# A transformer-like stack on one core: the same operations in another written-out order, with buffers handed out in order of release

## The chip, the cores and the metric

The kernel runs on one core of a Trainium2 chip. The metric is the time of one execution on the device, in microseconds (us); the median of several runs counts. One execution of the kernel before was also taken by the hardware profiler, and all rows shown come from that one.

## The reference

Four layers in a row over x of 2048 tokens by 512, all in float32:

```python
def A(x, wqkv, wo):                # 32 heads of 16; window of 8 tokens, every second one back
    q, k, v = split((x @ wqkv))    # 512 -> 3 * 512
    logits[s, w] = q[s] . k[s - 2*w] * 16**-0.5     (s - 2*w < 0 is masked)
    return (softmax(logits) weighted sum of v[s - 2*w]) @ wo

def B(x, w1, w2, w3, w4):
    h = gelu(layernorm(x) @ w1)
    # the four quarters of h's columns are shifted by +1, -1, +2, -2 tokens
    x1 = x + shifted(h) @ w2
    return x1 + gelu(layernorm(x1) @ w3) @ w4       # 512 -> 1792 -> 512

x = x + A(layernorm(x));  x = x + B(layernorm(x))
x = x + A(layernorm(x));  x = x + B(layernorm(x))
```

## The kernel before

**Tiles.** The tokens are cut into 4 blocks of 512, each of 4 tiles of 128. With two passes through A and B there are 8 units, numbered n = 0 to 7. For each unit the program has the stages p1 (normalize x, transpose it, multiply by wqkv, write q, k and v to DRAM), p2 (load q, and k and v with their windows, and do the attention on VectorE: products of 128x2048, reductions, softmax, sums), p3 (multiply by wo, normalize, transpose, multiply by w1, Gelu, shift), p4 (multiply by w2, normalize, transpose) and p5 (the wide MLP in 14 slices: up by w3, Gelu, down by w4 into accumulators). Stages of neighbouring units overlap.

**Precision.** Most products are done on pairs of float16: each operand is a rounded part and a rest, and three products (high by high, high by rest, rest by high) stand for one. So a typical operation on TensorE is a group of 12 matmuls of 128x512. Splitting a tile into the two parts is what much of the work on ScalarE (ACT), VectorE (DVE) and GpSimd (POOL) is: a copy to float16, then a subtraction. In the wide MLP a bank of products is read by three such steps: the Gelu in place (`mm<-mm,s_w`), the high part (`g<-mm,c_g`), and the rest, either on DVE (`g<-mm,c_g,g`) or by a copy on ACT (`f<-mm,c_g`) and a subtraction on POOL.

**The chain of a transposed tile.** A normalization takes a sum of squares on ACT, three tiny steps on POOL (tile `small`, 128x1), the scaling on ACT, the split on ACT and DVE or POOL, and a transposing DMA issued by SP, the queue of nearly all transfers. Only then can TensorE multiply the tile.

**Banks.** PSUM has 8 banks of 128x512, four called `mm` (for products that are evicted at once) and four called `acc` (for sums over many slices). A new group of matmuls into an `mm` bank waits until all steps that read its previous contents are done. The other buffers (`x`, `kv`, `q`, `f32`, `ev`, `g`, `w` and so on) are handed out in the same way from pools of 1 to 11.

**Order.** The program first builds a list of 3513 operations (class `Graph`), each with its engine or a choice of two engines, its estimated cost, what it reads and writes, and the buffers it touches. Nothing of the order is left to a scheduler: `PLACES[k]` is the place of the k-th operation built in one list for all engines, and `OTHER` names the operations that use their second engine. `plan` walks the list in that order, gives each operation its buffers, and the instructions are then issued in it; a helper keeps each engine's instructions in program order. So an engine whose next instruction waits holds up all that stand behind it in its queue. All instructions are issued from one line (L354), so rows of the profile are told apart by their tiles, not by lines.

In the kernel before, `plan` also carries a model of the engines (start times, delays, a port that VectorE and GpSimd share, DMA lanes, table loads, a cold TensorE), whose only use is the choice of buffers: of the free ones it takes that which, by the model, was released first.

Of the kernel before, what the change touches and what calls it, by code (L numbers as in the profile page):

```python
# [227 lines left out]
class Graph:  # L228
# [3 lines left out]
    def __call__(self, key, alts, r=(), w=(), after=(), xfer=0.0, late=0.0):  # L232
# [34 lines left out]
        return o  # L267


LAT, LAT_PE, LAT_SP, LAT_DMA, LEAD, TABLE, COLD = 0.06, 0.35, 0.15, 1.5, 0.85, 1.3, 1.0  # L270
TAIL = (0.165, 0.085, 0.115, 0.0, 0.0)
FREE = (6.5, 1.0, 0.72, 1.2, 0.72)
LANES = 8
GRANT, HELD, SMALL = 0.14, 0.4, ("tiny", "root")
BY_DMA = {"p1": 1, "p2": 1, "p3": 1, "p4": 0}


def plan(ops, slots):
# [9 lines left out]
    for o in sorted(ops, key=lambda o: o.key):  # L288
        assert o.n == 0, "an operation stands before one that it needs"
        e, d, o.fn, cls = o.alts[OTHER.get(o.seq, 0)]  # L290
        begin = o.est
# [1168 lines left out]
```

## Time and profile before

| | |
|---|---|
| median of 3 runs | 1149.2 us (1148.75 to 1150.22) |
| the profiled execution's own time | 1149.52 us |
| its span, first to last instruction | 1147.7 us |
| mean granted TensorE clock | 0.995 |
| TensorE busy | 1121.6 us, 98% |
| VectorE, ScalarE, GpSimd busy | 77%, 54%, 43% |
| DMA | 207.16 MB, mean 180 GB/s |

Busy time is the union of an engine's instructions; a busy TensorE need not run at its peak. "Idle before" is the time in which the engine had nothing to run, and the name behind the arrow is what ended it. A wait for several things is put down to the one that came last.

### The profile page before, as it was taken

The numbers are of one execution on the slowest core, as the hardware profiler recorded it, in microseconds if no ns is written. First come the engines' busy times: TensorE is split into PE (matmuls) and PEld (weight loads), VectorE is DVE, ScalarE is ACT, GpSimd is POOL, SyncE is SP. The second block draws the span as 40 slices with busy tenths as digits, with TensorE's granted clock in tenths as the row PEclk, the third lists the DMA queues.
The fourth block names the chain that finished last, engine by engine and source line by source line (L and its number), as shares of the span: only waits on it lengthen the run. The fifth ranks groups of instructions, "written<-read, shape, count | busy, mean of one in ns | idle before, by whom it ended". The sixth has DMA issues, their size and how long they took to land.

```text
span 1147.7 us, 15205 instructions
## 1 busy us (share of the span) xinstructions
PE 1121.6 (98%) x5236; PEld 526.5 (46%) x5236; DVE 880.8 (77%) x914; ACT 617.6 (54%) x1077; POOL 489.9 (43%) x619
## 2 busy tenths in 40 slices
PE   8999998998999999999999899999999999999998
PEld 6554444443444444444444344444444444444544
DVE  3999999988998998887889787777877989423212
ACT  4975884257754476365554556463545545545322
POOL 4656584156423455255535323444545342324000
PEclk9999999999999999999999899999999999999999
DMA  7789999998988579974488649884767567434323
GB/s 221 192 215 230 244 260 252 239 219 221 241 230 205 116 193 204 243 195 119 108 218 201 158 112 243 197 211 126 170 175 208 154 152 188 110 83 83 102 83 101
DMA packets 247101, 207.16 MB, mean 180 GB/s; under 512 B 134344, under 2 KB 188616, under 8 KB 247024
## 3 DMA queue, kind: packets, MB, share of 16 engines
q1 hardware_dynamic: 245408, 204.42, 71.2%
q10 hardware_dynamic: 1616, 1.77, 0.5%
q8 instruction: 41, 0.67, 0.3%
q14 instruction: 36, 0.29, 0.1%
HBM read 132.64 MB, written 37.87 MB: 149 GB/s over the span
## 4 chain that ended last, share of the span: by engine, by line
PE 55%; DVE 18%; POOL 8%; issue 7%; ACT 6%; DMA 5%; SPq 1%; POOLq 0%; DVEq 0%; ACTq 0%
PE mm L354 38%; PE acc L354 17%; DVE prod L354 10%; POOL small L354 4%; DVE L L354 3%; ACT f L354 2%; ACT junk L354 1%; SPq L354 1%; DMA kv<-kv_d 1%; DVE x L354 1%; POOL f L354 1%; DVE f L354 1%; DVE mx L354 1%; DVE g L354 1%; DMA w<-in_A_x_dram 1%
## 5 line engine op out<-in xcount | busy, mean ns | idle before, releaser
L354 PE MATMUL acc<-w,g 128*128 128x512 f16 (+1 forms) x1260 | 308.3, 393 | 2.0 <-DVE g L354 0.5
L354 PE MATMUL mm<-nT,w 128*128 128x512 f16 (+1 forms) x1344 | 293.5, 372 | 2.1 <-DVE g L354 1.1
L354 PE MATMUL mm<-wq_hl,xt 128*128 128x512 f16 x1008 | 230.4, 384 | 10.3 <-ACT f L354 3.4
L354 PEld LDWEIGHTS <-w 128*128 128x128 f16 x1512 | 141.2, 98 | 158.6 <-issue 7.3
L354 POOL TENSOR_SCALAR small<-small 128x1 f32<-128x1 f32 (+1 forms) x204 | 120.2, 590 | 158.2 <-ACT junk L354 147.0
L354 ACT ACTIVATE mm<-mm,s_w 128x512 f32<-128x512 f32 (+1 forms) x144 | 90.0, 627 | 174.3 <-PE mm L354 173.9
L354 PEld LDWEIGHTS <-g 128*128 128x128 f16 x1176 | 114.5, 98 | 140.4 <-DVE g L354 2.7
L354 DVE TENSOR_TENSOR prod<-kv,L 128x2048 f32<-128x2048 f32 x64 | 150.0, 2344 | 14.6 <-POOL o L354 10.3
L354 PEld LDWEIGHTS <-xt 128*128 128x128 f16 x1008 | 99.2, 99 | 132.3 <-issue 14.7
L354 DVE TENSOR_REDUCE L<-prod 128x128 f32<-128x2048 f32 x64 | 146.0, 2282 | 1.1
L354 DVE TENSOR_TENSOR prod<-kv,q 128x2048 f32<-128x2048 f32 x58 | 139.6, 2407 | 4.2 <-DMA kv<-kv_d 2.6
L354 DVE TENSOR_TENSOR prod<-prod 128x1024 f32<-128x1024 f32 (+1 forms) x114 | 121.5, 1068 | 5.3 <-ACT prod L354 2.8
L354 DVE SCALAR_TENSOR_TENSOR g<-mm,c_g,g 128x512 f16<-128x512 f32 x56 | 41.5, 746 | 78.2 <-ACT g L354 78.1
L354 PE MATMUL mm<-nT,w_hl 128*128 128x512 f16 x384 | 87.2, 380 | 1.8 <-DVE mx L354 1.8
L354 PE MATMUL mm<-w_hl,h 128*128 128x512 f16 x384 | 86.1, 379 | 0.4 <-POOL h L354 0.2
L354 POOL TENSOR_TENSOR g<-f,g 128x512 f16<-128x512 f32 x31 | 48.6, 1569 | 84.7 <-ACT f L354 42.0
L354 PE MATMUL mm<-wo_hl,oT 128*128 128x512 f16 x336 | 74.2, 379 | 0.0
L354 POOL TENSOR_TENSOR small<-small,nhalf 128x1 f32<-128x1 f32 (+1 forms) x104 | 71.1, 684 | 6.3
L354 POOL TENSOR_TENSOR prod<-prod 128x512 f32<-128x512 f32 x17 | 23.9, 1408 | 104.6 <-DVE prod L354 104.6
L354 ACT ACTIVATE g<-mm,c_g 128x512 f16<-128x512 f32 x98 | 66.5, 684 | 2.0
L354 PEld LDWEIGHTS <-oT 128*128 128x128 f16 x426 | 41.4, 98 | 50.4 <-DVE oT L354 1.2
L354 PEld LDWEIGHTS <-w_hl 128*128 128x128 f16 x384 | 37.6, 99 | 48.0 <-issue 4.2
(196 smaller groups left out, 1253.3 us busy)
## 6 DMA issues: line engine op xcount, KB each, us to landing
w<-w SPq DMA_DIRECT2D x210, 256.0 KB
kv<-kv_d SPq DMA_DIRECT2D x112, 352.0 KB
kv_d<-ev SPq DMA_DIRECT2D x112, 128.0 KB
w<-in_B_w_dram SPq DMA_DIRECT2D x42, 256.0 KB
q_d<-ev SPq DMA_DIRECT2D x28, 256.0 KB
w<-g SPq DMA_DIRECT2D x28, 256.0 KB
q<-q_d SPq DMA_DIRECT2D x28, 256.0 KB
x<-x SPq DMA_DIRECT2D x26, 256.0 KB
```

The source lines that it names most:

```text
L354: i = f(*a, **k).ins
```

## The change

Both lists are replaced, and `plan` loses its model: a buffer that is released goes to the end of its pool's list, and the next operation that needs one takes the first of that list. The new lists come from a search outside the program with an event-driven picture of the engines and of the port that VectorE and GpSimd share. No operation is added, removed or resized. 94 of the 3513 operations keep their place in the list. `OTHER` goes from 137 to 151 entries. 132 operations change engine:

| from | to | operations |
|---|---|---|
| DVE | POOL | 51 |
| POOL | DVE | 54 |
| ACT | POOL | 15 |
| POOL | ACT | 9 |
| DVE | ACT | 2 |
| ACT | DVE | 1 |

Of the operations that follow in the text, with their place in their engine's own queue:

| operation | what it is | engine | place before | place after |
|---|---|---|---|---|
| 45 | centring the fourth input tile | POOL, then DVE | 12 | 8 |
| 1278 | product for the wide MLP, unit 1 | PE | 143 | 143 |
| 1639 | tiny normalization step, p4 of unit 2 | POOL | 248 | 260 |
| 1651 | tiny normalization step, p4 of unit 2 | POOL | 251 | 257 |
| 1652 | scaling that reads it | ACT | 388 | 381 |
| 1778 | product by wqkv, unit 5 | PE | 190 | 190 |
| 1823 | copy that frees its bank before | ACT | 390 | 389 |
| 1448 | copy that frees its bank after | ACT | 395 | 385 |
| 1862 | exponential of the attention, unit 5 | ACT | 531 | 531 |
| 2105 | product for the wide MLP, unit 3 | PE | 260 | 259 |
| 2106, 2107, 2108 | Gelu, high part and copy of it | ACT | 532, 533, 534 | 523, 528, 524 |
| 2177 | product by wqkv, unit 6 | PE | 263 | 260 |

The diff, without the two lists' numbers:

```diff
 PLACES = [int(k) for k in """
-49 22 56 77 23 195 3 4 0 1 8 11 14 7 17 19 24 35 36 29 5 16 31 32
...
+68 40 21 101 52 171 3 0 2 1 17 13 19 15 24 26 53 35 29 28 4 8 9 10
...
 def plan(ops, slots):
-    free, latest = list(FREE), {}
-    lane, lanes = 0, [0.0] * LANES
-    pool = {k: [(0.0, j) for j in range(len(v))] for k, v in slots.items()}
-    for o in ops:
+    pool = {k: list(range(len(v))) for k, v in slots.items()}
+    order = sorted(ops, key=lambda o: o.key)
+    for o in order:
         for kind, j in o.lend:
-            pool[kind].remove((0.0, j))
...
-    for o in sorted(ops, key=lambda o: o.key):
+            pool[kind].remove(j)
+    for o in order:
         assert o.n == 0, "an operation stands before one that it needs"
-        e, d, o.fn, cls = o.alts[OTHER.get(o.seq, 0)]
-        begin = o.est
+        o.fn = o.alts[OTHER.get(o.seq, 0)][2]
         for b in o.touch:
             if b.slot is None:
-                got = min(pool[b.kind])
-                pool[b.kind].remove(got)
-                begin, b.slot = max(begin, got[0]), got[1]
+                b.slot = pool[b.kind].pop(0)
                 b.t = slots[b.kind][b.slot]
-        begin = max(begin, free[e])
...
         for kind, j in o.lend:
-            pool[kind].append((o.end + LAT, j))
+            pool[kind].append(j)
         for b in o.touch:
-            latest[b] = max(latest.get(b, 0.0), o.end)
             b.left -= 1
             if b.left == 0:
-                pool[b.kind].append((latest[b] + LAT, b.slot))
+                pool[b.kind].append(b.slot)
```

More of the change, by code (lines that the diff above doesn't have):

```diff
@@ L267, in __call__ @@
         return o
[L270 to L274, printed above, removed]
 BY_DMA = {"p1": 1, "p2": 1, "p3": 1, "p4": 0}
 def plan(ops, slots):
-    free, latest = list(FREE), {}
-    lane, lanes = 0, [0.0] * LANES
-    pool = {k: [(0.0, j) for j in range(len(v))] for k, v in slots.items()}
-    for o in ops:
+    pool = {k: list(range(len(v))) for k, v in slots.items()}
@@ L285, in plan @@
+    order = sorted(ops, key=lambda o: o.key)
+    for o in order:
         for kind, j in o.lend:
-            pool[kind].remove((0.0, j))
-    dma_free, port, wide, table, order = 0.0, 0.0, 0.0, None, []
-    for o in sorted(ops, key=lambda o: o.key):
+            pool[kind].remove(j)
+    for o in order:
         assert o.n == 0, "an operation stands before one that it needs"
-        e, d, o.fn, cls = o.alts[OTHER.get(o.seq, 0)]
-        begin = o.est
+        o.fn = o.alts[OTHER.get(o.seq, 0)][2]
@@ L292, in plan @@
         for b in o.touch:
             if b.slot is None:
-                got = min(pool[b.kind])
-                pool[b.kind].remove(got)
-                begin, b.slot = max(begin, got[0]), got[1]
+                b.slot = pool[b.kind].pop(0)
                 b.t = slots[b.kind][b.slot]
-        begin = max(begin, free[e])
-        if o.xfer:
-            begin = max(begin, *(lanes[(lane + k) % LANES] for k in range(o.parts)))
-            free[e] = begin + d
-            dma_free = max(dma_free, begin + d + LEAD) + o.xfer
-            o.end = dma_free + LAT_DMA + o.late
-            for k in range(o.parts):
-                lanes[lane] = o.end
-                lane = (lane + 1) % LANES
-        else:
-            if e == ACT and cls is not None and cls != table:
-                table = cls
-                d += TABLE
-            if e == POOL:
-                if begin < port:
-                    begin = max(begin, port - GRANT)
-                wide = max(wide, begin) if cls in SMALL else begin + d - GRANT
-            elif cls == "lock":
-                begin = max(begin, wide)
-                port = begin + d
-            if e == PE and begin - free[PE] > COLD and begin > 20.0:
-                d += min(begin - free[PE] - COLD, 2.5)
-            o.end = begin + d + (TAIL[PE] if e == PE else 0.0)
-            free[e] = o.end - TAIL[e]
-            if cls == "root":
-                o.end += HELD
@@ L324, in plan @@
-        order.append(o)
         for s in o.succ:
-            g = s.alts[0][0]
-            s.est = max(s.est, o.end + (LAT if e == g else LAT_PE if g == PE else LAT_SP if g == SP else LAT))
             s.n -= 1
         for kind, j in o.lend:
-            pool[kind].append((o.end + LAT, j))
+            pool[kind].append(j)
         for b in o.touch:
-            latest[b] = max(latest.get(b, 0.0), o.end)
             b.left -= 1
             if b.left == 0:
-                pool[b.kind].append((latest[b] + LAT, b.slot))
+                pool[b.kind].append(b.slot)
```

305 rows, old and new, of tables (OTHER, PLACES) are left out of this document.

## The prediction

> **What bounds the kernel now.** I read the busy shares first, then the table by stretches, then TensorE's own timeline, and last the queues of the engines that its waits name.
>
> The page's first parts (engine, busy us, share of the span, instructions; below, the granted TensorE clock in tenths):
>
> ```profile
> span 1147.7 us, 15205 instructions
> PE 1121.6 (98%) x5236; PEld 526.5 (46%) x5236; DVE 880.8 (77%) x914; ACT 617.6 (54%) x1077; POOL 489.9 (43%) x619
> PEclk9999999999999999999999899999999999999999
> ```
>
> TensorE is the bound: 1121.6 of 1147.7 us, and no product is added or taken away. A new order can win only TensorE's idle time, 26.1 us, and time lost to a low clock; it can lose much more. The stretches show where the idle time lies (stretch, length, then busy us and instructions of PE, PEld, DVE, ACT, POOL, granted clock, DMA share, GB/s):
>
> ```profile
> 0.00:20.00 20.00, 16.17 (x92) 12.91 (x93) 8.24 (x22) 6.51 (x14) 10.57 (x31) 1.00 0.85 251
> 20.00:160.00 140.00, 138.05 (x619) 70.44 (x618) 127.35 (x139) 110.23 (x230) 86.31 (x96) 1.00 0.87 223
> 160.00:180.00 20.00, 17.27 (x73) 7.21 (x72) 19.93 (x27) 16.10 (x26) 15.59 (x22) 0.93 0.88 224
> ...
> 260.00:300.00 40.00, 36.09 (x162) 16.05 (x161) 35.10 (x54) 32.58 (x60) 26.97 (x37) 1.00 0.83 215
> ...
> 440.00:480.00 40.00, 37.49 (x173) 16.62 (x171) 35.39 (x31) 19.72 (x31) 16.27 (x14) 1.00 0.95 219
> ...
> 620.00:660.00 40.00, 36.64 (x158) 15.83 (x157) 30.70 (x26) 21.06 (x32) 17.89 (x19) 0.91 0.64 149
> 660.00:1140.00 480.00, 479.64 (x2339) 221.71 (x2338) 294.75 (x308) 228.96 (x380) 166.62 (x221) 1.00 0.58 147
> 1140.00:1147.70 7.70, 3.24 (x24) 1.57 (x21) 3.27 (x6) 0.71 (x2) 0.00 (x0) 0.93 0.57 170
> ```
>
> Idle are 20 − 16.17 = 3.83 us at the start and 7.70 − 3.24 = 4.46 at the end; so 26.1 − 3.83 − 4.46 = 17.8 us lie between 20 and 1140, of which only 0.36 after 660. The whole second half is full already. Single waits, from TensorE's timeline (start, length, what, count, idle time before it and what ended that):
>
> ```profile
> 17.22 0.66 PE L354 MATMUL mm<-ident,f 128*128 128x128 f32 x4 [1.51 <-POOL f L354]
> ...
> 176.79 7.04 PE L354 MATMUL mm<-wq_hl,xt 128*128 128x512 f16 x24 [2.38 <-DMA xt<-f]
> 184.86 6.01 PE L354 MATMUL mm<-nT,w 128*128 128x384 f16 x36 [1.02 <-ACT ev L354]
> ...
> 267.54 10.52 PE L354 MATMUL mm<-nT,w_hl 128*128 128x512 f16 x48 [1.62 <-DVE mx L354]
> ...
> 320.47 5.34 PE L354 MATMUL mm<-nT,w 128*128 128x512 f16 x24 [1.07 <-DVE g L354]
> ...
> 445.02 5.34 PE L354 MATMUL mm<-wq_hl,xt 128*128 128x512 f16 x24 [1.74 <-ACT ev L354]
> ...
> 638.98 5.28 PE L354 MATMUL mm<-wq_hl,xt 128*128 128x512 f16 x12 [3.36 <-ACT f L354]
> 644.05 3.15 PE L354 MATMUL mm<-nT,w_hl 128*128 128x512 f16 x12
> 647.03 2.75 PE L354 MATMUL mm<-nT,w 128*128 128x512 f16 x12
> ```
>
> An undisturbed group of twelve takes 2.75 us, two take 5.34. After the wait of 3.36 us the next groups took 5.28 and 3.15: 2.53 + 0.40 = 2.93 us lost to the clock (granted 0.91 in that stretch); after the wait of 2.38 the next two took 7.04, 1.70 too much (0.93). After 1.74, 1.62 and 1.07 nothing is lost. So the ceiling is 17.8 + 2.93 + 1.70 = 22.4 us, and at the start no more than 3.83; the last products and the last stores stand alike in both orders.
>
> The Trainium skill ("TensorE: Matmul & The Clock Gate", Part 1, What's actually happening) has the clock halve after an idle window of about 3.4 us and come back after as long a busy one, the window running freely. The wait of 3.36 us agrees; the one of 2.38 is shorter than a window and lost 1.70 all the same, which only the free running allows. If a wait of that length usually cost nothing in clock, the sum below would be 0.85 us poorer (half of 1.70); nothing else hangs on this.
>
> **The change part by part.** All operations are kept; numbers below are those in the order in which the program builds them, places are counted in an engine's own queue by walking both lists. Three things move. (1) Order: of TensorE's 476 operations 258 places hold another one, but blocks only swap with near neighbours. DVE, ACT, POOL and SP are reshuffled at over 90% of places, mostly by a few. (2) 132 operations change engine: 51 from DVE to POOL, 54 back, 15 from ACT to POOL, 9 back, 3 between ACT and DVE. (3) Buffers, PSUM banks above all, go to the next user in the order in which the program releases them, no longer by the planner's release times.
>
> *The wait of 3.36 us at 638.98* (operation 2177). Its bank had belonged to product 2105, whose three ACT steps came last in this queue:
>
> ```profile
> 629.89 0.81 ACT L354 ACTIVATE f<-x,small 128x512 f32<-128x512 f32 x1 [3.43 <-POOL small L354]
> 630.61 0.64 ACT L354 ACTIVATE mm<-mm,s_w 128x512 f32<-128x512 f32 x1
> ...
> 633.73 1.28 ACT L354 ACT_TABLE_LOAD   x1
> ...
> 635.67 1.28 ACT L354 ACT_TABLE_LOAD   x1
> 636.97 0.66 ACT L354 ACTIVATE mm<-mm,s_w 128x512 f32<-128x512 f32 x1
> ...
> 638.25 0.68 ACT L354 ACTIVATE f<-mm,c_g 128x512 f32<-128x512 f32 x1
> ...
> 619.47 0.74 DVE L354 SCALAR_TENSOR_TENSOR x<-mm,s_wo,x 128x512 f32<-128x512 f32 x1
> ```
>
> The product had long been done, but the softmax exponential stood before its Gelu and brought two table loads. In the new queue that Gelu has place 523, not 532, right behind the Gelu of 630.61 and ahead of the exponential (531); its last copy has 524, not 534. And operation 2177 gets another bank, freed by the DVE step of 619.47, done by 620.2; the bank of 2105 goes to a product one group later. The wait should go with its clock loss: −3.36 − 2.93 = **−6.3 us**. What is late next are the normalized tiles of block 4 whose ACT steps now stand behind the Gelu; TensorE meets them at once (the row of 644.05). That goes into the term for new waits.
>
> *The wait of 1.74 at 445.02 and that of 1.07 at 320.47:*
>
> ```profile
> 437.13 4.30 POOL L354 TENSOR_SCALAR small<-small 128x1 f32<-128x1 f32 x3
> ...
> 442.92 0.81 ACT L354 ACTIVATE f<-f,small 128x512 f32<-128x512 f32 x1 [1.11 <-POOL small L354]
> ...
> 444.30 0.67 ACT L354 ACTIVATE ev<-mm,s_kv 128x512 f32<-128x512 f32 x1
> ...
> 306.50 0.69 ACT L354 ACTIVATE ev<-mm,s_kv 128x512 f32<-128x512 f32 x1 [0.38 <-PE mm L354]
> ```
>
> At 445.02 the bank is freed by the copy of 444.30, queued behind the step of 442.92, which waits for POOL. In the new order the longest piece of that POOL stretch (operation 1639) goes from place 248 to 260, behind the step that ACT waits for (257), and another copy frees the bank, at ACT's place 385 instead of 390: **−1.74**. At 320.47 the bank is now one freed by the copy of 306.50, some 12 us early: **−1.07**.
>
> *260 to 300:* idle 40 − 36.09 = 3.91, of it 1.62 at 267.54. The steps in front move by little both ways, and one bank is reused one product earlier; I take half, −1.9, between 0 and −3.9.
>
> *176.79 and 184.86:* 2.38 + 1.70 + 1.02 = 5.1. The first waits for a transposing DMA that stands behind other transfers in SP's queue; its place goes from 180 to 181, and the transfers ahead wait for a DVE step that has place 136, not 144. I take half, −2.5, between 0 and −5.1.
>
> *The start and the moves between engines:*
>
> ```profile
> 11.65 0.49 DVE L354 TENSOR_SCALAR f<-w,mx 128x512 f32<-128x512 f32 x1
> ...
> 15.12 2.04 POOL L354 TENSOR_SCALAR f<-w,mx 128x512 f32<-128x512 f32 x1
> ...
> L354 POOL TENSOR_TENSOR prod<-prod 128x512 f32<-128x512 f32 x17 | 23.9, 1408 | 104.6 <-DVE prod L354 104.6
> ...
> L354 DVE TENSOR_TENSOR prod<-prod 128x512 f32<-128x512 f32 x48 | 35.8, 747 | 1.1
> ```
>
> The step of 15.12, which TensorE awaits for 1.51, goes to DVE, where its like took 0.49: −1.5 (between 0 and −3.8, all that is idle there; another of its kind goes to POOL). The other moves nearly cancel: 51 against 54 change DVE's load by about 3 × 0.75 = 2 us, beside TensorE; I cost them at nothing, since DVE is idle for 480 − 294.75 us after 660, and up to their own 2 us where DVE is full (19.93 of 20 at 160).
>
> *Small waits elsewhere:* 17.8 − 3.36 − 1.74 − 1.07 − 3.91 − 3.40 = 4.3 us, taken as they are. *New waits* are not in this trace: at least 0, at most all that is saved and some more. I take one like that at 176.79 with its clock loss (4.1) and one like that at 320.47 (1.1), 5.2 in all, since a product meets an eviction within one group about as often: among the longer kinds of eviction, three engine steps, I count 9 such reuses of a bank after one product in between, before 12.
>
> Sum: −6.3 − 1.7 − 1.1 − 1.9 − 2.5 − 1.5 + 5.2 = **−9.8 us**. The profiled execution took 1149.5 (span and 1.8 around it), the median is 1149.2: 1149.5 − 9.8 = 1139.7, so **1140 us**.
>
> **The rivals.** *As many new waits as old ones*: the new order is also planned ahead, and a misjudged step anywhere stops TensorE. For it: nearly every place on four queues is new, and bank reuse is hardly looser. Against it: the five largest waits each have a cause that the lists remove. Then the 15.0 us of the terms above come back, 1149.
>
> The Trainium skill ("Perfetto Trace Analysis", Optimizing Scalar/DVE Operations) says that GpSimd and VectorE share a read port, so that shifting work between them might not help. The pair 1408 against 747 ns and the 2.04 us step agree that POOL pays for it; by the rule alone the term at the start would be 0 and the time 1141, within the forecast's case.
>
> *Slower*: POOL's small steps in front of the first MLP block, at 174 us, get 8.8 us more POOL work ahead of them (17.1 in, 8.3 out, by the planner's costs). If that made them late, the wait at 184.86 would grow by 8.8 and lose 2.93 to the clock; with the −2.5 lost as well, −9.8 + 2.5 + 8.8 + 2.9 = +4.4, 1154. It decides from a delay of some 4.4 us on. Against it: POOL idles 140 − 86.31 = 53.7 us before, and after 140 us more is taken out than put in.
>
> *All waits vanish*: −22.4 − 1.5, 1126; against it, four queues are fed by transfers whose landing no order fixes.
>
> **How the numbers follow.** About 0.2% (2.3 us) is what a measurement of this kernel can tell from no change. Chances: the forecast 0.50, all waits vanish 0.10, as many new waits 0.27 (half of it within 0.2%, a third slower, the rest faster), slower by POOL 0.13. Faster 0.50 + 0.10 + 0.05 = 0.65, same 0.13, slower 0.09 + 0.13 = 0.22. The likeliest case's own range: new waits of 0 and both halves won give −9.8 − 5.2 − 4.6 = −19.6, 1130; new waits twice as large and no halves −9.8 + 5.2 + 4.4, 1149. For 8 in 10 the upper end reaches toward the POOL case: 1130 to 1153.
>
> **What would show it.** Right: PE busy 3 to 5 us lower (no clock loss at 640 and 177), mid idle near 10 us, no wait over 2 us between 600 and 660, 445 without its wait. Wrong: a granted clock under 0.95 in a new slice, TensorE waiting for POOL `small` or a transposed tile around 160 to 200, or new waits for `mm` banks after 660, where none were.

## The result, and the profile after

The changed kernel takes 1133.2 us (median of 4 runs, 1128.9 to 1136.1) against 1149.0 for the kernel before in the same comparison: ratio 0.986, 95% interval 0.9827 to 0.9894. Beside the experiments it was run again: 1133.2 (5 runs), ratio 0.9865 (0.9845 to 0.9886). The forecast was 1140, with a range of 1130 to 1153. The profiled execution took 1133.4 us, with a span of 1131.6, 16.1 less than that of before.

The first part of the page, and the stretches (same columns as in the prediction):

```profile
span 1131.6 us, 15180 instructions
...
0.00:20.00 20.00, 16.49 (x84) 13.03 (x85) 8.10 (x20) 6.04 (x14) 9.87 (x25) 0.91 0.90 250
20.00:160.00 140.00, 136.27 (x611) 69.97 (x610) 127.47 (x135) 107.69 (x225) 97.22 (x109) 1.00 0.86 218
160.00:180.00 20.00, 17.19 (x82) 7.77 (x81) 19.90 (x24) 15.40 (x27) 16.07 (x23) 1.00 0.99 263
180.00:260.00 80.00, 79.81 (x337) 39.75 (x336) 76.41 (x76) 33.71 (x63) 24.91 (x29) 1.00 0.92 229
260.00:1124.00 864.00, 862.35 (x4112) 395.77 (x4111) 638.01 (x659) 448.35 (x745) 331.98 (x436) 1.00 0.69 170
```

Behind 180 us TensorE hardly stands: 0.19 us to 260, and 1.65 in the 864 us from there to 1124. Four waits behind 185 were named for the kernel before: those at 638, 445 and 320, and the 3.91 us between 260 and 300. They are gone but for 0.26 us at 275, and nothing of their size has come in their place. Ahead of 180 it is no better than before: 20 to 160 lost 140 − 136.27 = 3.73 us instead of 1.95.

A table cut at the start of the wide MLP's first product (184.86 and 184.87 us in the two kernels) says it most plainly. First the kernel before, then the changed one:

```profile
0.00:184.86 184.86, 175.32 (x795) 92.02 (x796) 160.10 (x190) 135.02 (x272) 115.02 (x147) 0.99 0.87 225
```

```profile
0.00:184.86 184.86, 174.62 (x794) 92.72 (x795) 160.19 (x182) 132.40 (x268) 125.82 (x158) 0.99 0.89 226
```

Up to that product both have run the same 85 operations of TensorE in the same time (the counts differ by one record). So all 16.1 us lie behind it. There the kernel before has 1147.7 − 184.86 = 962.8 us with 1121.6 − 175.3 = 946.3 busy, idle 16.5. The changed one has 946.7 us with 1115.1 − 174.6 = 940.5 busy, idle 6.2. Idle time gave 10.3 us, and the four named waits make 3.36 + 1.74 + 1.07 + 3.91 = 10.1. Busy time gave 5.8, of which 2.93 are the slow products behind 638.98. About half of the other 2.9 is the tails of groups: a group of twelve counts as 2.75 us busy before a wait, and as 2.59 when the next one follows at once. Behind the first product the kernel before has 12 waits and the changed one 3, and 9 × 0.16 = 1.4. For the rest there is no row.

TensorE's own timeline has what is left of waits over 0.7 us, apart from the very first and last:

```profile
9.18 0.66 PE L315 MATMUL mm<-ident,f 128*128 128x128 f32 x4 [1.79 <-POOL f L315]
...
179.32 5.35 PE L315 MATMUL mm<-wq_hl,xt 128*128 128x512 f16 x24 [2.81 <-DMA xt<-f]
184.87 4.06 PE L315 MATMUL mm<-nT,w 128*128 128x384 f16 x24 [0.19 <-DMA nT<-f]
```

Besides these there are 1.64 at 98 us (for POOL's attention output), 1.19 at 121 (for a transposed tile) and 1.00 at 549. The start's wait has only changed owner: operation 45 went to VectorE, but operation 24, the same step on the first tile, went to POOL and took 2.02 us there. The clock of the first 20 us came out lower too (0.91, before 1.00); the prediction had named a new slow slice as a sign against it, and here it lies where nothing was won. The wait at 179, for a transposed tile, is another of those signs. It is longer than its forerunner (2.38), but the two groups behind it took 5.35 us, the undisturbed time.

And ACT's queue around the Gelu that had been late (operations 2106 and 2108 are the rows of 619.08 and 619.77):

```profile
619.08 0.66 ACT L315 ACTIVATE mm<-mm,s_w 128x512 f32<-128x512 f32 x1 [1.41 <-PE mm L315]
619.77 0.69 ACT L315 ACTIVATE f<-mm,c_g 128x512 f32<-128x512 f32 x1
...
624.09 1.28 ACT L315 ACT_TABLE_LOAD   x1
625.38 0.63 ACT L315 ACTIVATE L<-L 128x512 f32<-128x512 f32 x1
```

It runs as soon as its product is there, 18 us earlier than before, and the exponential with its table load follows.

### The profile page after: what moved, and what is told of

It is laid out like the page before. It is cut to its first block, busy times and chain, and to the rows that moved or that the text cites. A ratio compares the mean times of both kernels' runs of the same rounds, so it can differ in the third digit from the quotient of the medians.

```text
span 1131.6 us, 15180 instructions
## 1 busy us (share of the span) xinstructions
PE 1115.1 (99%) x5236; PEld 527.6 (47%) x5236; DVE 872.9 (77%) x915; ACT 611.9 (54%) x1073; POOL 480.1 (42%) x620
## 4 chain that ended last, share of the span: by engine, by line
PE 81%; DVE 6%; DMA 3%; ACT 3%; POOL 3%; issue 1%; SPq 0%; ACTq 0%; DVEq 0%; POOLq 0%
PE mm L315 58%; PE acc L315 24%; DVE prod L315 3%; DMA kv<-kv_d 2%; POOL small L315 1%; DMA xt<-f 1%; ACT junk L315 1%; DVE L L315 1%; ACT f L315 1%; POOL g L315 0%; DVE x L315 0%; ACT x L315 0%; DVE g L315 0%; ACT wq_hl L315 0%; POOL prod L315 0%
## 5 line engine op out<-in xcount | busy, mean ns | idle before, releaser
L315 PE MATMUL mm<-wq_hl,xt 128*128 128x512 f16 x1008 | 225.9, 379 | 4.8 <-DMA xt<-f 4.6
L315 DVE TENSOR_TENSOR prod<-kv,q 128x2048 f32<-128x2048 f32 x58 | 138.2, 2382 | 10.1 <-DMA kv<-kv_d 5.8
L315 POOL TENSOR_SCALAR small<-small 128x1 f32<-128x1 f32 (+1 forms) x204 | 95.4, 468 | 118.8 <-ACT junk L315 106.2
L315 POOL TENSOR_TENSOR g<-f,g 128x512 f16<-128x512 f32 x35 | 51.6, 1480 | 77.3 <-ACT f L315 34.1
L315 POOL TENSOR_TENSOR small<-small,nhalf 128x1 f32<-128x1 f32 (+1 forms) x104 | 81.2, 782 | 6.0
L315 ACT ACTIVATE ev<-mm,s_kv 128x512 f32<-128x512 f32 x56 | 37.7, 682 | 43.8 <-DMA kv_d<-ev 18.4
```

What stands on the lines that cost most here:

```text
L315: i = f(*a, **k).ins
```

## The experiments

My theory after the result: the gain comes from the places of the operations in the queues. Rivals: it comes from the way buffers are given out, or from the engines chosen. The first four runs cross the three parts of the change. The next ones do a single move in one of the two kernels, to see whether a wait has a price of its own. Operations are named by their numbers in building order; a move in the list rewrites `PLACES`, and nothing else.

**The new lists with the old way of giving out buffers.**

```diff
-def plan(ops, slots):            # first in, first out
+def plan(ops, slots):            # the old one, by modelled release times
```

> The new order and the new engines, but buffers given out by the planner's release times as before. Theory (the places in the queues do it, the buffer rule does nothing of size): the banks of the products that stood at 638.98, 445.02 and 320.47 come out the same under both rules, so none of those waits returns; 1134 us, between 1130 and 1138, no wait of TensorE over 3 us in the middle. Rival (the buffer rule does it): most of the 15.8 us come back, 1145 to 1150, with a wait for an mm bank of 2 us or more between 300 and 660.

1133.8 us, ratio 0.9872 (0.9855 to 0.9888). As the theory had it: with the new lists the rule for buffers makes no difference that can be told. The rival falls.

**The old lists with the new way of giving out buffers.**

```diff
-def plan(ops, slots):            # by modelled release times
+def plan(ops, slots):            # first in, first out
```

> The old order and the old engines, with buffers given out first in, first out. Theory (places): the wait of 3.36 us behind the softmax exponential and that of 1.74 at 445 stand again; 1149 us, between 1146 and 1153. Rival (buffer rule): 1133 to 1138, and those two waits are gone.

1164.2 us, ratio 1.013 (1.0115 to 1.0146). Neither theory had that: the two waits stand, as expected (2.53 us at 451 and 2.43 at 650), but the time is 16 us longer than before. ACT's timeline shows where it comes from:

```profile
304.39 0.67 ACT L314 ACTIVATE ev<-mm,s_kv 128x512 f32<-128x512 f32 x1
308.87 0.81 ACT L314 ACTIVATE f<-f,small 128x512 f32<-128x512 f32 x1 [3.81 <-DMA nT<-f]
...
438.82 0.81 ACT L314 ACTIVATE f<-x,small 128x512 f32<-128x512 f32 x1 [2.93 <-DMA xt<-f]
```

A normalization is given an `f` tile that a transposing DMA still reads. First in, first out goes by the order in which the list lets buffers go, and a DMA that stands early in the list ends late. With the old rule the same step began at 304.05, without a wait. TensorE then stands 3.30 us at 323 and 3.96 at 468, for steps queued behind these. Matched product by product with the kernel before, it is 10.6 us late at 500 us and 14.8 at the end. What is lost after 500 us was not followed row by row, though two more such waits for transposing DMAs stand on ACT there (2.06 us at 701, 2.24 at 947). So the rule is not free. The new lists fit it, the old ones don't.

**The new order with the old engines.**

```diff
-OTHER = ...    # 151 entries, the new list
+OTHER = ...    # 137 entries, the list of before; PLACES and plan stay new
```

> The new order and the new buffer rule, but every operation on the engine it had before (132 move back). Theory (places): the waits of 638, 445 and 320 stay away, the first centring step is on VectorE again (its wait of 1.79 us goes), but queues were ordered for the other engines, so some small waits appear; 1136 us, between 1131 and 1142. Rival (engines do it): 1146 to 1150.

1184.5 us, ratio 1.0307 (1.0283 to 1.0331): 51 us slower than the changed kernel, and slower than before. Here my theory was wrong, and so was its rival in that form. Two rows of VectorE and one of TensorE show one of the places:

```profile
125.43 4.48 DVE L314 TENSOR_TENSOR prod<-kv,L 128x2048 f32<-128x2048 f32 x2
129.84 0.68 DVE L314 TENSOR_TENSOR f<-f,f 128x512 f16<-128x512 f32 x1
```

```profile
133.71 6.66 PE L314 MATMUL mm<-wq_hl,xt 128*128 128x512 f16 x24 [5.67 <-DMA xt<-f]
```

The rest of a split (682, 129.84 us) had its input from ACT's step of 119.28, but on VectorE it stands in the list behind the attention's products, and it starts some 10 us late. In the new lists it belongs to POOL. There, in the changed kernel, it ran at 112.89 us, and POOL stood idle for 2.20 us before it and for 4.96 behind it. The loads of the two engine lists hardly differ (VectorE busy 874.0 us here and 872.9 in the changed kernel, GpSimd 489.4 and 480.1); the places are made for one of them.

**The old order with the new engines.**

```diff
-OTHER = ...    # 137 entries, the list of before
+OTHER = ...    # 151 entries, the new list; PLACES and plan stay old
```

> The old order and the old buffer rule, with the new engines. Theory (places): the exponential still stands before the Gelu, so the wait near 638 stands, and POOL steps come at places made for VectorE; 1151 us, between 1147 and 1157. Rival (engines do it): 1134 to 1140.

1156.1 us, ratio 1.0063 (1.0048 to 1.0078). As the theory had it, with the wait at 641.62 grown to 4.62 us. The four runs together: alone, neither the order nor the engines win anything (36 and 8 us slower than before); together they win some 15, with either rule for buffers. So the theory of the places is half right: what the places win, they win only with the engines they were made for. Two mixtures were not run: the new order with the old engines and the old rule, and the old order with the new engines and the new rule.

**The kernel before with the exponential behind the Gelu.**

```diff
 # the list, by operation numbers
-2365 2356 2366 1861 1891 1862 ... 2106 ... 2107 2108 2177
+2365 2356 2366 1861 1891 ... 2106 ... 2107 2108 1862 2177
```

> The kernel before with one operation moved: the softmax exponential of the attention unit stands behind the three ACT steps of the Gelu, not ahead of them; all buffers are given out as before. Theory (the wait of 3.36 at 638.98 and its clock loss of 2.93 came from this one place): the wait is under 0.5 us, granted clock 1.00 in the stretch 620 to 660, 1142.5 us, between 1140 and 1145, all of it still there at the end since nothing waits after 660. Rival (the wait moves on): the next products, on the normalized tiles of block 4, wait instead, and 1146 to 1150 comes out.

1148.4 us (10 runs), ratio 1.0007 (0.9997 to 1.0017). The rival holds. TensorE's and VectorE's timelines:

```profile
638.78 2.75 PE L354 MATMUL mm<-nT,w_hl 128*128 128x512 f16 x12 [0.69 <-DMA nT<-f]
...
649.43 2.75 PE L354 MATMUL mm<-wq_hl,xt 128*128 128x512 f16 x12 [2.72 <-DVE g L354]
```

```profile
646.42 2.29 DVE L354 TENSOR_TENSOR prod<-kv,L 128x2048 f32<-128x2048 f32 x1 [0.84 <-POOL o L354]
648.63 0.74 DVE L354 SCALAR_TENSOR_TENSOR g<-mm,c_g,g 128x512 f16<-128x512 f32 x1
```

The wait of 3.36 is gone, but 0.69 us stand at the next product and 2.72 some 11 us behind that, 3.41 in all. The second is the wait of product 2197 for its bank. The step that frees it (2116, the row of 648.63) has its input at 645.5 and stands behind attention sums on VectorE. While TensorE was held up by ACT, it came too late to notice.

**The same, and that step of VectorE moved ahead of the sums.**

```diff
 # on top of the move above
-1867 1868 1869 1870 2116
+1867 2116 1868 1869 1870
```

> The kernel before with two operations moved: the exponential behind the Gelu as in the run with one move, and VectorE's gated product, which TensorE then awaited for 2.72 us at 649.43, ahead of the attention sums that stood in front of it. Theory (a wait behind one queue covered a wait behind the next; both queues have to be changed): no wait over 1 us between 620 and 660, and 2.7 us less than with one move alone, 1145.5 us, between 1143.5 and 1147. Rival (the stretch is held by still another chain): a third wait within 20 us, 1147.5 to 1149.

1145.8 us (11 runs), ratio 0.9981 (0.9972 to 0.999). The theory holds to 0.3 us: no wait over 0.7 us stands between 620 and 660 (39.32 of 40 us busy), and 2.6 us are won by the medians. The traces agree: matched product by product, TensorE gains 2.9 us between 630 and 655 on the kernel with one move. Two queues had to be changed for one wait; the second move without the first was not run.

**The kernel before with the eviction of 445 moved up.**

```diff
 # ACT's queue, by operation numbers
-1640 1641 1652 1653 1823
+1640 1641 1823 1652 1653
```

> The kernel before with one operation moved: the eviction that TensorE awaits at 445.02 goes ahead of the layer-norm step in front of it on ACT, which idles 1.11 us there for a POOL step, so the copy costs that step nothing; four other buffers out of 1305 are given out differently. Theory (each wait is its own term, and later stretches keep the gain): that wait goes, -1.7, 1146.8 us, between 1145.5 and 1148. Rival (the stretch up to 480 is held by something else, and the next product waits longer): no change, 1148 to 1149.5, with a larger wait at 461.

1146.8 us (10 runs), ratio 0.9989 (0.9978 to 1.0): the figure expected, but the interval touches no change. In the trace 1778 starts at 442.92 with a wait of 0.24 for its tile; 0.68 at 451.55 and 1.19 at 460.67, where 0.41 and 0.36 stood before, bring back 1.1 of the 1.5 us that were won. So the median speaks for the theory and the trace for its rival, a longer wait at 461: the question stays open, and that the figure was met is no proof. The same trace, with the wait for the exponential still in it:

```profile
637.94 2.75 PE L354 MATMUL mm<-wq_hl,xt 128*128 128x512 f16 x12 [3.34 <-ACT f L354]
```

It is the wait of 3.36 of the kernel before, and the group behind it took 2.75 us, not 5.28.

**The changed kernel with the transposing DMA of 179 us issued early.**

```diff
 # the list, by operation numbers
-846 225 222 ... 1142 ... 1036 847
+846 847 225 222 ... 1142 ... 1036
```

> The changed kernel with one operation moved: the transposing DMA that TensorE awaits for 2.81 us at 179.32 is issued right behind the POOL step that makes its data, no longer 9.7 us later. Theory (a chain holds this stretch): that wait goes, but the MLP's first product at 184.87 waits for its own transposed tiles, whose chain does not get shorter (ACT, POOL and DVE steps from 175 on, last issue 181.59, landing at about 184.8), so some 2.5 to 3.0 us of waiting stand there instead, and the time stays at 1133, between 1131 and 1136. Rival (waits add up): -2.8, 1130.4, and the wait at 184 stays at 0.2.

1134.0 us, ratio 0.9881 (0.9865 to 0.9897), against 1133.2 without the move. The theory holds:

```profile
171.32 7.93 PE L315 MATMUL mm<-wq_hl,xt 128*128 128x512 f16 x36
185.60 5.65 PE L315 MATMUL mm<-nT,w 128*128 128x384 f16 x24 [6.34 <-DMA nT<-f]
```

Three groups run without a gap, and then TensorE waits for the MLP's tiles, which come no earlier (185.60, before the move 184.87). I had 2.5 to 3.0 us; it was 6.34, because TensorE reached that product earlier than in the first trace (its first stretch had gone better), and the tiles came 0.7 later. The two groups behind that wait took 5.65 us instead of 4.06, a clock loss of 1.6.

**The changed kernel with the first centring step on VectorE.**

```diff
-OTHER = {24, 108, 111, ...}
+OTHER = {108, 111, ...}
```

> The changed kernel with the first centring step on VectorE, as before the change, no longer on POOL (2.02 us there, 0.48 on VectorE). Theory (a chain of VectorE and transposes holds TensorE until 185): the wait of 1.79 at 9.18 falls under 0.5, TensorE stands longer at 179 or 185, and the end stays at 1133, between 1131.5 and 1135. Rival (the start's gain lasts): -1.5, 1131.7, and the product of 184.87 begins 1.5 us earlier.

1130.7 us (4 runs, 1128.9 to 1132.0), ratio 0.9851 (0.9834 to 0.9868). The figures are the rival's: no wait for this tile is left, and the MLP's first product begins at 181.75, 3.1 us earlier. (The trace is of the fastest of the four executions.)

```profile
174.87 7.04 PE L315 MATMUL mm<-wq_hl,xt 128*128 128x512 f16 x24 [2.96 <-DMA xt<-f]
181.75 4.06 PE L315 MATMUL mm<-nT,w 128*128 128x384 f16 x24
```

So the chain that ends in the MLP's tiles is not a fixed date: here, and in the kernel with two mends below (182.68), it ends earlier when the start's wait is gone. That what is won ahead of TensorE's products moves the whole chain is a reading and not shown: in the run with the early transpose TensorE was 2.4 us ahead of the changed kernel's first trace at 98 us, and the tiles still came 0.7 later.

**Two mends in the changed kernel, and more TensorE work ahead of the MLP.** Three kernels ran on one chip: the one with the step above and two POOL steps moved up (to take away the wait at 98 us), that one with the early transpose and one more product in front of the MLP, and the changed kernel itself.

```diff
 # first: operation 24 out of OTHER, and in POOL's queue
-802 803 ... 413 414
+413 414 802 803
 # second: besides, 847 behind 846; product 871 from 867th place in the list to just ahead of 1070,
 # its eviction 872 and stores 873, 874 behind 1077, stores 877, 878 behind 1067
```

> The changed kernel with the first centring step on VectorE again, and the two POOL steps that end in the attention output of 98 us ahead of the two layer-norm steps that stood before them; all buffers as in the changed kernel. Theory (waits before 160 us feed the chains behind them, so what is won there is kept): both waits, 1.79 and 1.64, go; 1129.8 us, between 1128 and 1132. Rival (the chain to 185 takes the second gain back): 1131 to 1133, as with the first centring step alone.

> The two mends, the transposing DMA of 179 issued early, and one more projection product of 2.6 us (with its eviction and its four stores or their place in SP's queue) brought forward from about 237 us to just ahead of the MLP's first product at 185, to fill the wait that the early transpose left there. Theory (that wait is a chain, and only other work for TensorE fills it): 2.6 us less than with the two mends alone, 1127.2, between 1125.5 and 1130. Rival (the store issues brought forward delay weights and tiles on SP's queue, or the product is missed at 237): no gain or a loss, 1130 to 1134.

> The changed kernel itself, beside the two mended ones on the same chip. Both theories: 1133 us, between 1131 and 1135; waits near 9, 98 and 179 as in its first trace. If the clock's losses depend on when a wait falls, 7.0 us for the two groups behind the wait near 179 in some executions, 5.35 in others.

1130.8 us (1130.3 to 1131.5, ratio 0.985, 0.9835 to 0.9865) with the two mends; 1144.1 (ratio 0.9962, 0.9952 to 0.9972) with the product brought forward; 1133.2 for the changed kernel. The two mends give what the first alone gave (1130.7). That is the rival's claim, though 1130.8 lies in the theory's range and just under the rival's, and the reason is not the one I named. The two mended POOL steps, on POOL and what ran beside them on VectorE:

```profile
89.86 1.27 POOL L315 TENSOR_TENSOR prod<-prod 128x512 f32<-128x512 f32 x1
91.21 2.66 POOL L315 TENSOR_TENSOR o<-prod 128x256 f32<-128x256 f32 x1
```

```profile
89.94 3.35 DVE L315 TENSOR_TENSOR prod<-kv,x 128x2048 f32<-128x2048 f32 x1 [0.89 <-POOL o L315]
93.31 2.29 DVE L315 TENSOR_REDUCE L<-prod 128x128 f32<-128x2048 f32 x1
```

The same step of POOL and the same product of VectorE in the changed kernel:

```profile
97.27 0.73 POOL L315 TENSOR_TENSOR o<-prod 128x256 f32<-128x256 f32 x1
```

```profile
93.55 2.29 DVE L315 TENSOR_TENSOR prod<-kv,x 128x2048 f32<-128x2048 f32 x1 [0.89 <-POOL o L315]
```

The last step took 2.66 us instead of 0.73, ending 0.6 us after VectorE's product, so a wait of 1.51 stayed at TensorE (1.64 before the mend); and 2.25 came at 104 us, for a bank whose step stands in VectorE's queue.

In the kernel with the product brought forward, that product does fill its place (44 matmuls without a gap from 171.72 on), but SP's queue pays:

```profile
184.44 0.54 SPq L315 DMA_DIRECT2D w<-in_B_w_dram  x1
191.79 1.25 SPq L315 DMA_DIRECT2D kv_d<-ev  x2
```

```profile
184.41 3.10 PE L315 MATMUL mm<-nT,w 128*128 128x384 f16 x12 [3.02 <-DMA nT<-f]
...
204.86 5.01 PE L315 MATMUL acc<-w,g 128*128 128x512 f32 x6 [6.00 <-DMA w<-in_B_w_dram]
```

The stores brought forward wait for their eviction on ACT, which stands behind the MLP's second product; SP issues nothing for 6.8 us, and the weights behind it come late: 6.00 us at 204.86. The rival's direction holds, far beyond its size: 13.3 us. Between 180 and 260 us TensorE was busy for 68.7 us, against 79.6 with the two mends alone.

The kernels with one and with two mends have medians 2.5 and 2.4 us below the changed one and are the fastest by their medians; the intervals of their ratios overlap with the changed kernel's, so their lead over it is not settled.

## Why the prediction was right, and where it was not

The direction, the mechanism and the place of most of the gain came as forecast. The size was 6.3 us short on the profiled executions (9.8 against 16.1), and two misses of opposite sign kept it from being worse: 4.0 us of forecast gain at the start and up to 185 did not come, and 5.2 of forecast new waits did not come either. That these nearly cancel is luck.

- *The waits at 638, 445 and 320* are gone, each with the bank that the lists named. Their sum of 9.1 us with the clock loss is what the trace of before shows. But the first term's price was not one of its own: in the kernel before, taking that wait away at its cause won nothing (1.0007), because the next wait stood some 11 us behind it. With VectorE's step moved too it won 2.6 us. The change also avoids that second wait, but in another way. In VectorE's queue step 2116 still stands behind the sums; it is product 2197 that goes from place 267 to 262 of TensorE's queue, ahead of the product whose bank 2116 frees, so that it no longer waits for that bank. That this was needed the prediction did not see, though it named what to look for ("What is late next"). The waits at 320 and from 260 to 300 were not taken away one by one, and that at 445 stays open.
- *The clock loss of 2.93* belongs to that execution: the same wait of 3.34 us, in the kernel with the copy moved, lost nothing. As part of a median it was priced too high.
- *260 to 300* gave all but 0.26 of its 3.91 us, where I took half.
- *The start and the stretch to 185* gave 0 instead of −1.5 − 2.5 = −4.0: both kernels begin the MLP's first product at the same time, with the same matmuls done. The step that failed is the sum of waits in that stretch. The wait at 179 hides the wait for the MLP's tiles, as the early transpose showed; taking half of such a pair was not a bound on it. The kernel before with the eviction of 445 moved up, which has the order of the kernel before up to there, shows the same:

```profile
174.97 5.35 PE L354 MATMUL mm<-wq_hl,xt 128*128 128x512 f16 x24 [1.56 <-DMA xt<-f]
183.78 6.01 PE L354 MATMUL mm<-nT,w 128*128 128x384 f16 x36 [3.45 <-DMA nT<-f]
```

The first wait is shorter than in the kernel before and loses no clock, and the second is 3.45 us instead of 1.02: TensorE was 1.0 us ahead at 173 us and is 1.1 ahead at the MLP's first product. So the 1.70 of clock there had no price either.

At the start I saw operation 45 leave POOL and noted that another of its kind goes there, but did not cost it: it took 2.02 us, TensorE waited 1.79, and the eight products behind that wait took 3.62 us, where they took 1.99 in the run with the early transpose. Putting it back is worth 2.5 by the medians, which is not settled. That "the five largest waits each have a cause that the lists remove" was a wrong reading for two of them: the transposed tile's wait at 177 and the start's stand again as 2.81 and 1.79.

- *New waits* were the term that was mis-sized: +5.2 beside the 4.3 of small waits kept. Behind 184.86 the changed kernel stands 6.2 − 4.6 (its end) = 1.6 us in all; before, 16.5 − 4.5 − 10.1 = 1.9 stood there besides the named waits. New and old small waits nearly cancel there. In front of it idle time grew by 1.8 between 20 and 160. My count of bank reuses priced a risk that the new lists avoid.
- *Moves between engines at nothing* had a wrong reason. I argued by totals (51 against 54, VectorE idle after 660); but the moves have no price of their own. In the new order they are worth 51 us, in the old one they cost 8: what counts, in the place followed, is which queue stands free there.
- *The rule for buffers*: I looked at PSUM banks alone. With the new lists that was enough (1133.8 with the old rule, 1133.2 with the new). The old lists lose 16 us to it, as far as it was followed by `f` tiles under transposing DMAs.
- *The rival by POOL's small steps* before the MLP did not come: the product stands at 184.87, as before.

## What to carry to other kernels

A wait at the bound engine is worth its length only if the next queue is ready earlier too: look up what the following products would have waited for, and move that as well, or give the product another bank. Places, engine choices and the rule for buffers of a written-out order are one plan, and a part of it put into another plan can cost more than the whole brings. Work brought forward brings its evictions and stores with it, and in a queue that serves everything they hold up what stands behind them.

## What the runs showed of the hardware

**The clock.** Waits of like length lose clock time in one execution and none in another. Two groups of twelve behind the wait at 179 take 5.35 us undisturbed; the rows are those of the changed kernel run again, and of the kernel with two mends:

```profile
178.90 7.04 PE L315 MATMUL mm<-wq_hl,xt 128*128 128x512 f16 x24 [4.18 <-DMA xt<-f]
```

```profile
177.15 5.35 PE L315 MATMUL mm<-wq_hl,xt 128*128 128x512 f16 x24 [3.44 <-DMA xt<-f]
```

After 2.81 and 3.44 us nothing was lost, after 2.38, 2.96 and 4.18 some 1.7 us each time; after 3.36 the loss was 2.93, after 3.34 nothing. The Trainium skill ("TensorE: Matmul & The Clock Gate", Part 1, What's actually happening) has a free-running window of about 3.4 us, idle to fall to half the clock and busy to come back; a loss of 1.7 us is half of one such window, an estimate from that page. The free running would fit that like waits differ, but no run here shows where a window begins. That 2.38 and 2.96 us are enough does not follow from a wholly idle window, and free running does not explain it either, as the prediction had it: a wait shorter than the window cannot hold a whole one. There the measurement decides. So a clock loss read from one execution is a draw, and goes into a forecast with a chance.

**POOL beside VectorE.** One and the same POOL step took 0.73 and 2.66 us, and the product of VectorE beside it 3.35 instead of 2.29. The Trainium skill ("SBUF — State Buffer", Who interferes with whom) says that a VectorE instruction with two inputs in SBUF and a GpSimd instruction that reads SBUF exclude each other; this trace agrees, in both directions: VectorE's product, begun at 89.94, lost about 1.1 us to the POOL step that ran until 91.13, and the next POOL step ended only after that product. The pair 1408 against 747 ns that the prediction set beside a shared port shows mainly that POOL is slower at this step: beside a reduction of VectorE it took 1.26 us in the changed kernel (95.93). I had not priced the sharing in moving the two steps: a move on POOL needs a look at VectorE's row beside it.
